# Linear attention and a gated feed-forward on one core: the later pairs' query projection as one block in four banks

## The chip, the core and the metric

The program runs on one core of a Trainium2 chip. The time of a kernel is the device time of that core in microseconds (us); the kernel before takes 1162.48 us, the median of three runs (1160.75 to 1164.28). The core has a matrix engine (TensorE, PE in the profile), a vector engine (VectorE, DVE), a scalar engine (ScalarE, ACT), GpSimd (POOL) and SyncE (SP), whose queue issues almost all DMAs, in order.

## The reference

Eight batches, eight heads, 576 tokens, head size 64. The features are exponentials of a projection on 128 columns, less its largest absolute value; the attention is linear in them. Its output, 4608 tokens of 512, goes through a gated feed-forward with 1536 hidden units.

```python
def phi(x):                                    # w_phi: 64 x 128
    proj = np.einsum('bhsd,df->bhsf', x, w_phi)
    proj = proj - np.max(np.abs(proj), axis=-1, keepdims=True)
    return np.concatenate([np.exp(proj), np.exp(-proj)], axis=-1)
q_p, k_p = (phi(q), phi(k))
kv = np.einsum('bhsf,bhsd->bhfd', k_p, v)
num = np.einsum('bhsf,bhfd->bhsd', q_p, kv)
den = np.einsum('bhsf,bhf->bhs', q_p, np.sum(k_p, axis=2))[..., None] + 1e-06
x = (num / den) as 4608 x 512
out = (silu(x @ w_gate) * (x @ w_val)) @ w_out
```

## The kernel before

**Work.** The attention goes by pairs of heads: 32 pairs, four to a batch. Pairs 0 to 11 are "early", pairs 12 to 31 "later" (this change touches these). A later pair has four pieces of PE work, called K, q, V and N below:

- K (lines 562, 565): the projection of the pair's keys, nine products of 128 columns. A head takes one half of the array's rows, so products of the two heads go side by side; the keys' last 64 tokens of both heads are the ninth product (line 565), on the first half of the rows. It takes three of the eight PSUM banks. DVE then takes the maximum and subtracts it (lines 573, 579), ACT makes the two exponentials (line 584).
- q (line 705): the projection of the queries, 288 columns for each head and half of the tokens. Each half is a step of its own: two products, two banks. ACT copies them out (line 710); DVE turns them, takes maxima and subtracts (714 to 738), ACT makes the exponentials (740, 742).
- V (601, 594): the sum over the keys, with the array split in two halves of columns. It needs the exponentials of K.
- N (760): the numerators and the denominator of the queries. ACT, DVE (770 to 782) divide and turn the result into the tile `turned`; four DMAs for every two pairs store it in DRAM (`x_dram`, line 794).

**The feed-forward** goes by 12 chunks c of 384 tokens. Chunks 0 to 3 are computed plainly (line 389 on PE). From chunk 4 on two chunks are done together by Strassen's scheme: seven products in place of eight (line 1214). For that `operands(c)` loads the attention's output back from `x_dram` into `stage` (line 1162), and ACT and DVE make of it seven split operands `tb` (1172, 1173, 1178); the first two are the tokens of chunk c alone, the third product of a step (operand 5) needs chunk c+1 as well. Chunk 4 begins with tokens of batches 2 and 3, so it needs pairs 12 to 15; chunk 7, the partner of chunk 6, needs pairs 20 to 23.

**Order.** A planner (class `Plan`) writes the program's order out: each step has an engine, a cost, what it waits for and the banks that it takes (`take`) and gives back (`give`). A step is taken when it is ready and as many banks are free as it takes; else it is held and the next one by key gets its turn. The order of instructions on every engine and on SP's queue is what comes out. While PE would wait in the plan, a product on an idle tile is put in (lines 1408 to 1413), in the feed-forward only while a sum over hidden units is open. The engines then run their queues strictly in that order. In the plain chunks two banks are held for the first layer and three for the second (`gv_names`, `begin_sums`), so three are free; when the first layer of chunk 3 is done the two are let go. In Strassen's steps four banks are held.

The functions that the change touches, and what calls them:

Of the kernel before, what the change touches and what calls it, by code (L numbers as in the profile page):

```python
# [17 lines left out]
P = 128  # L18
S = 576
SH = S // 2  # L20
NBL = S // 32
D = 64
NF = 128
# [54 lines left out]
class Plan:  # L78
# [21 lines left out]
    def add(self, eng, cost, fn, after=(), rank=0.0, take=None, give=None, mode="whole"):  # L100
        port = eng in ("DVE2", "POOL")
        eng = eng[:3] if eng == "DVE2" else eng
        s = Step(eng, cost, fn, rank, len(self.steps), self.LAG[eng], take, give, (rank, len(self.steps)))
        s.port = port
        s.slack = self.SLACK.get(eng, 0) if 16 <= rank < 1000 and cost > 1 else 0
        s.mode = mode if eng == "PE" and cost > 1 else None
        seen = set()
        for a in after:
            if a is not None and id(a) not in seen:
                seen.add(id(a))  # L110
                a.then.append(s)
                s.left += 1
        self.steps.append(s)
        return s
# [146 lines left out]
def dve(n):  # L261
    return 150 + 1.04 * n
# [10 lines left out]
def act(n):  # L273
    return 190 + 0.86 * n
# [6 lines left out]
def pe32(n):  # L281
    return 2 * max(112, 0.85 * n)
# [3 lines left out]
def favor_attention_moe(ctx: ExitStack, tc: tile.TileContext, qT, kT, v, w_phi, wg, wv, wo, out):  # L286
    nc = tc.nc
# [11 lines left out]
    def sb(name, shape, dtype=F32, n=None):  # L299
        if n is None:  # L300
            return pool.tile(shape, dtype, name=name, tag=name)
        return [pool.tile(shape, dtype, name=f"{name}{i}", tag=f"{name}{i}") for i in range(n)]
# [17 lines left out]
    kin, qin = sb("kin", [P, KW]), [sb("qin", [P, KW]), ahead.rearrange("p n c -> p (n c)")[:, :KW].bitcast(F32)]  # L320
# [4 lines left out]
    qx = [sb("qx0", [P, 2, S]), sb("qx1", [P, 2, S])]  # L325
# [3 lines left out]
    qy = sb("qy", [P, 4, NF], F32, 2)  # L329
# [20 lines left out]
    def bank(name):  # L350
        return banks.tile([P, 512], F32, name=name, tag=name)

    work = [bank(f"work{i}") for i in range(8)]
# [3 lines left out]
    wst = sb("wst", [P, NF])  # L357
# [9 lines left out]
    plan = Plan(len(work))  # L367
    add = plan.add
# [99 lines left out]
    def rows(h):  # L468
        return slice(h * D, h * D + D), slice((1 - h) * D, (1 - h) * D + D)
# [44 lines left out]
    last = {}  # L514

    def attention(i, rank):
        b, pr = divmod(i, NPAIR)
        early = i < EARLY_PAIRS
        j = i % 2
        jq = j if early else 0  # L520
        vec = nc.vector

        use = lambda name: [last.get((name, i - 2))]
# [8 lines left out]
        q_in = [add("SP", P * q_width * 4, lambda: nc.sync.dma_start(qin[jq][:, :q_width], qT[b, pr, :, :q_width]), q_free, rank)]  # L532
        if early:
            q_in.append(add("SP", 2 * D * D * 4, lambda: nc.sync.dma_start(side(qin[jq]), ends(qT)), q_free, rank))
        n = 4 * P * P
# [11 lines left out]
        for g, (t0, t1) in enumerate(K_GROUPS):  # L547
            both = t0 == 4
            w = t1 - t0
            heads = 1 if both else 2  # L550
            m2 = w * heads
            n = m2 * NF
            by_head = not both
            key = ("k", i, g)
            view = lambda key=key, n=n: work[plan.bank[key]][:, :n].rearrange("p (t f) -> p t f", f=NF)

            def project(t0=t0, t1=t1, key=key, heads=heads, both=both):
                projected.append(1)
                if not both:
                    for t in range(4):  # L560
                        for h in range(2):
                            nc.tensor.matmul(work[plan.bank["k", i, h]][:, t * NF:(t + 1) * NF],  # L562
                                             kin[rows(h)[0], t * P:(t + 1) * P], wst[rows(h)[0]], start=True, stop=True)
                if both or not early:
                    nc.tensor.matmul(work[plan.bank["k", i, 2]][:, :NF], kin[:D, 4 * P:], wst[:D], start=True, stop=True)  # L565

            if both and early:
                kproj = add("PE", pe32(NF), project, [*k_in, kproj], rank, take=key, mode="rows")
            elif not g:
                kproj = add("PE", (4 if early else 5) * pe32(NF), project, [*k_in, last.get(("kp", i - 1, 0))], rank,  # L570
                            take=[("k", i, n) for n in range(2 if early else 3)], mode="rows")
            m = km[(3 * i + g) % len(km)]
            kmax = add("DVE", dve(n), lambda m2=m2, m=m, view=view: vec.tensor_reduce(
                out=m[:, :m2], in_=view(), axis=AX.X, op=ALU.max, apply_absolute_value=True),
                       [kproj, last.get(("km", 3 * i + g - 4))], rank)
            kpv = kp[g]

            def centre(m2=m2, m=m, view=view, kpv=kpv):
                vec.tensor_tensor(  # L579
                    out=kpv[:, :m2, 1], in0=view(), op=ALU.subtract,  # L580
                    in1=m[:, :m2].rearrange("p (n o) -> p n o", o=1).broadcast_to([P, m2, NF]))

            def exponential(s, m2=m2, kpv=kpv):
                nc.scalar.activation(kpv[:, :m2, s], kpv[:, :m2, 1], AF.Exp, scale=-1.0 if s else 1.0)  # L584

            ksub = add("DVE", dve(n), centre, [kmax, last.get(("kp", i - 1, g))], rank, give=key)
            e0 = add("ACT", act(n), lambda f=exponential: f(0), [ksub], rank)
            e1 = add("ACT", act(n), lambda f=exponential: f(1), [e0], rank)
            last["km", 3 * i + g] = ksub

            def values(kpv=kpv):
                for s in range(2):
                    for r in sides:
                        nc.tensor.matmul(ps_kv()[r, s * 2 * VD:(s + 1) * 2 * VD], kpv[:, 0, s, r],  # L594
                                         vl.rearrange("p h d -> p (h d)"), start=False, stop=s == 1)

            def values_of_head(h=g, kpv=kpv):
                for t in range(4):
                    for s in range(2):
                        for r in sides:  # L600
                            nc.tensor.matmul(ps_kv()[r, (2 * s + h) * VD:(2 * s + h + 1) * VD], kpv[:, t, s, r],  # L601
                                             vf[:, t, h], start=t == 0 and h + s == 0, stop=False)

            summed.append(values_of_head if by_head else values)
            made_keys.append(e1)
            if early:
                kv_steps.append(add("PE", 8 * KV_PACE if by_head else 2 * pe32(2 * VD), summed[-1],
                                    [e1, *v_in, *kv_steps[-1:]], rank, take=None if g else ("kv", i), mode="columns"))
                last["kp", i, g] = kv_steps[-1]
# [30 lines left out]
        if early:  # L640
            for g in range(3):
                tail = g == 2
                w = 1 if tail else 4
                n = 3 * i + g
                key, key2 = ("q", i, g), ("t", i, g)
# [12 lines left out]
                if tail:  # L658
                    pj = add("PE", pe32(NF), project, [*q_in, pj], rank, take=key, mode="rows")
                elif not g:  # L660
                    pj = add("PE", 4 * pe32(NF), project, [*q_in, *use("qx"), last.get(("qy", 3 * i - 1))], rank, take=[key, ("q", i, 1)], mode="rows")
# [34 lines left out]
                ahead_used.append(pj)  # L696
        else:
            copies = [[], []]
            pj = None
            for part, c in enumerate(halves):  # L700
                keys = [("q", i, h, part) for h in range(2)]

                def project(keys=keys, c=c):
                    for h in range(2):
                        nc.tensor.matmul(work[plan.bank[keys[h]]][:, :SH], wst[rows(h)[0]], qin[jq][rows(h)[0], c],  # L705
                                         start=True, stop=True)

                pj = add("PE", pe32(SH), project, [*q_in, pj, *use("qx"), last.get(("qy", 3 * i - 1))], rank, take=keys, mode="rows")
                for h in range(2):
                    copies[h].append(add("ACT", act(SH), lambda h=h, part=part, key=keys[h]: nc.scalar.copy(  # L710
                        qx[j][:, h].rearrange("p (n u s) -> p u n s", u=2, s=32)[:, part],
                        work[plan.bank[key]][:, :SH].rearrange("p (n s) -> p n s", s=32)), [pj, *use("qx")], rank, give=keys[h]))
            last["qin", i] = pj
            turns = [add("DVE", dve(S), lambda h=h: vec.transpose(qe[j][:, h], qx[j][:, h]),
                         [*copies[h], *use("qe")], rank) for h in range(2)]
# [596 lines left out]
    def attend(tokens):  # L1312
        while made[0] < min(NB * NPAIR, NPAIR * ((tokens + S - 1) // S)):
            attention(made[0], float(made[0]))
            made[0] += 1
        if late_sums:
            late_sums.pop()([])
# [42 lines left out]
    for f in range(NFT):  # L1360
# [3 lines left out]
        for c in range(EARLY):  # L1364
            j, h = first(c, f, low, 0)
# [18 lines left out]
    for f in range(NFT):  # L1384
        j, h = first(PLAIN - 1, f, low_parts(f, 0), 0)
# [80 lines left out]
```

## Time and profile before

| | |
|---|---|
| median of the runs shown | 1162.48 us |
| the profiled execution | 1161.04 us |
| its span, first to last instruction | 1159.2 us |
| PE busy | 1152.4 us (99%) |
| DVE, ACT, POOL busy | 793.7, 546.7, 139.6 us |
| DMA, share of the 16 engines' time (main queue) | 79.7% |

The profile is of one execution; it took 1.44 us less than the median of the runs. A PE that is busy for 99% of the span isn't one that works at its peak all that time: matmuls overlap each other in the records, so what one costs is read from the distance between two starts, not from its duration.

### The profile page before, as it was taken

To read this page: it belongs to the slowest core of one execution; us is meant where nothing else is said; L and a number is where in the kernel's file an instruction comes from. 1 tells how busy PE (TensorE), PEld (TensorE's weight loads), DVE (VectorE), ACT (ScalarE), POOL (GpSimd) and SP (SyncE) were. 2 spreads that over 40 slices of the span, in tenths; PEclk is the share of its full clock that TensorE was granted. 3 is DMA by queue.
4 is the path that set the end of the run, shared out by engine and by line. 5 is a ranking of instruction groups with operands and counts; after the bars stand their busy time and mean duration, and the time that the engine had idled before them with its cause. 6 is when DMAs were issued, how large, how long until landed. Compare 5 with 4: busy or idle time off the path is not lost.

```text
span 1159.2 us, 26379 instructions
## 1 busy us (share of the span) xinstructions
PE 1152.4 (99%) x9985; PEld 1015.2 (88%) x9985; DVE 793.7 (68%) x1573; ACT 546.7 (47%) x1233; POOL 139.6 (12%) x142
## 2 busy tenths in 40 slices
PE   9999999999999999999999999999999999999998
PEld 8777779999898888898987899898899998899986
DVE  7989899999567777477787455777536786534431
ACT  6887563333434555445455343554423553433332
POOL 1222300000122313010010001100001100001100
PEclk9999999999999999999999999999999999999999
DMA  5546678777799999997887788887888787889774
GB/s 170 178 144 197 220 254 289 249 261 263 268 313 297 326 298 359 340 307 233 243 281 235 252 274 288 239 255 245 264 267 272 246 248 232 270 284 304 246 222 159
DMA packets 220591, 298.32 MB, mean 257 GB/s; under 512 B 65840, under 2 KB 126384, under 8 KB 220464
## 3 DMA queue, kind: packets, MB, share of 16 engines
q1 hardware_dynamic: 220304, 296.57, 79.7%
q8 instruction: 79, 1.29, 0.5%
q14 instruction: 48, 0.39, 0.1%
q10 hardware_dynamic: 160, 0.07, 0.0%
HBM read 217.91 MB, written 78.64 MB: 256 GB/s over the span
## 4 chain that ended last, share of the span: by engine, by line
PE 86%; DVE 1%; DMA 1%; issue 0%; SPq 0%; ACT 0%; ACTq 0%
PE work L389 41%; PE work L1214 31%; PE work L760 4%; PE work L601 4%; PE work L705 2%; PE work L562 2%; PE work L594 1%; PE work L1413 1%; DMA w_lo<-wlo_dram 0%; DMA stage<-x_dram 0%; PE work L565 0%; PE work L817 0%; PE work L813 0%; PE work L677 0%; DVE qy L667 0%
## 5 line engine op out<-in xcount | busy, mean ns | idle before, releaser
L389 PE MATMUL work<-w_hi,hh 128*128 128x512 f32 x468 | 183.1, 399 | 0.0
L1236 DVE TENSOR_TENSOR m<-m,work 128x384 f32<-128x384 f32 x144 | 78.6, 552 | 117.7 <-ACT m L1233 67.8
L389 PE MATMUL work<-w_hi,m 128*128 128x512 f32 x396 | 156.7, 396 | 0.0
L382 DVE TENSOR_TENSOR m<-m,hh 128x384 fp32r<-128x384 f32 x132 | 74.8, 573 | 97.7 <-ACT hh L1002 85.8
L1002 ACT CAST hh<-m 128x384 fp32r<-128x384 f32 x144 | 73.3, 512 | 138.5 <-PE work L389 74.2
L389 PE MATMUL work<-xh,w_big 128*128 128x384 f32 x384 | 132.3, 345 | 0.0
L382 POOL TENSOR_TENSOR m<-m,m 128x384 f32<-128x384 f32 x48 | 58.7, 1223 | 590.5 <-DVE m L1241 296.1
L389 PE MATMUL work<-xl,w_big 128*128 128x384 f32 x384 | 128.6, 335 | 0.0
L1214 PE MATMUL work<-tb,stream_xh 128*128 128x384 f32 x618 | 115.3, 338 | 0.0
L1214 PEld LDWEIGHTS work<-tb,stream_xh 128*128 128x128 f32 x618 | 107.0, 188 | 4.7 <-issue 3.8
L389 PEld LDWEIGHTS work<-w_hi,hh 128*128 128x128 f32 x468 | 87.9, 188 | 21.5 <-issue 1.7
L1233 ACT COPY m<-work 128x384 f32<-128x384 f32 x144 | 68.0, 475 | 73.2 <-PE work L1214 71.0
L1240 ACT ACTIVATE m<-m 128x384 f32<-128x384 f32 x96 | 45.5, 517 | 110.2 <-DVE m L1236 109.5
L584 ACT ACTIVATE kp<-kp 128x512 f32<-128x512 f32 x128 | 78.5, 630 | 26.5 <-DVE kp L579 25.3
L389 PEld LDWEIGHTS work<-w_hi,m 128*128 128x128 f32 x396 | 74.4, 188 | 17.8
L1214 PE MATMUL work<-tb,stream_xl 128*128 128x384 f32 x468 | 88.9, 338 | 0.4 <-ACT m L1233 0.4
L1214 PEld LDWEIGHTS work<-tb,stream_xl 128*128 128x128 f32 x468 | 81.0, 188 | 4.0 <-issue 2.3
L389 PEld LDWEIGHTS work<-xh,w_big 128*128 128x128 f32 x384 | 72.2, 188 | 7.5 <-issue 4.4
L1214 PE MATMUL work<-tb,tb 128*128 128x384 f32 x408 | 77.8, 337 | 0.0
L601 PEld LDWEIGHTS work<-vf,kp 128*64 128x64 f32 x2048 | 62.6, 138 | 13.4 <-issue 5.5
L382 POOL TENSOR_TENSOR s<-s 128x256 f32<-128x256 f32 x48 | 41.3, 862 | 270.1 <-DMA s<-w_dram 231.7
L389 PEld LDWEIGHTS work<-xl,w_big 128*128 128x128 f32 x384 | 72.2, 188 | 1.0
(141 smaller groups left out, 2340.1 us busy)
## 6 DMA issues: line engine op xcount, KB each, us to landing
stream_xh<-wv_dram SPq DMA_DIRECT2D x103, 256.0 KB, 4.0
h_dram<-m SPq DMA_DIRECT2D x124, 192.0 KB, 3.8
m<-h_dram SPq DMA_DIRECT2D x124, 192.0 KB, 4.1
stream_xl<-wv_dram SPq DMA_DIRECT2D x78, 256.0 KB, 3.9
tb<-wv_dram SPq DMA_DIRECT2D x77, 256.0 KB, 4.1
w_lo<-wlo_dram SPq DMA_DIRECT2D x72, 256.0 KB, 4.2
stream_w_lo<-wv_dram SPq DMA_DIRECT2D x52, 256.0 KB, 3.9
stream_xl<-wlo_dram SPq DMA_DIRECT2D x48, 256.0 KB, 3.8
```

The costliest lines, as they stand in the source:

```text
L382: (nc.gpsimd if on == "POOL" else nc.vector).tensor_tensor(out=o, in0=a, in1=b, op=op)
L389: nc.tensor.matmul(o, l, r, start=a, stop=z)
L562: nc.tensor.matmul(work[plan.bank["k", i, h]][:, t * NF:(t + 1) * NF], kin[rows(h)[0], t * P:(t + 1) * P], wst[rows(h)[0]], start=True, st ...
L584: nc.scalar.activation(kpv[:, :m2, s], kpv[:, :m2, 1], AF.Exp, scale=-1.0 if s else 1.0)
L601: nc.tensor.matmul(ps_kv()[r, (2 * s + h) * VD:(2 * s + h + 1) * VD], kpv[:, t, s, r], vf[:, t, h], start=t == 0 and h + s == 0, stop=False)
L705: nc.tensor.matmul(work[plan.bank[keys[h]]][:, :SH], wst[rows(h)[0]], qin[jq][rows(h)[0], c], start=True, stop=True)
L760: nc.tensor.matmul(o[r, at:at + VD], features(k, h, slice(D * n, D * n + D)), kvs[j][:, (2 * k + h) * VD:(2 * k + h + 1) * VD], start=n % ...
L1002: s4 = add("ACT", act(CH), lambda: nc.scalar.copy(hh[b], th(j)), [made, hid_free[b]], FIRST)
L1214: nc.tensor.matmul(o(), l, r, start=begin and k + m == 0, stop=k + m == 3, skip_group_check=True)
L1233: return j, into(j, add("ACT", act(CH), lambda: nc.scalar.copy(th(j), src()), after, FIRST))
L1236: return add("DVE", dve(CH), lambda: vec.tensor_tensor(out=th(j), in0=th(j), in1=src(), op=ALU.add), after, FIRST)
L1240: s1 = into(t, add("ACT", act(CH), lambda: nc.scalar.activation(th(t), th(j), AF.Tanh, scale=0.5), [ready], FIRST))
```

## The change

For the later pairs the two steps of the query projection become one. It takes four banks (both heads, both halves) at once and issues eight products of 144 columns in place of four of 288, the heads in turn. The copies on ACT wait for the whole step and give back one bank each, as before. In the block of the keys the product of the last tokens goes first and the heads' order is turned round, so that the halves of rows still alternate. The early pairs keep their order. From line 716 on, line numbers of the changed kernel are three higher (1214 is 1217, 760 is 763, 794 is 797).

```diff
-            def project(t0=t0, t1=t1, key=key, heads=heads, both=both):
+            def project(both=both):
                 projected.append(1)
+                if both or not early:
+                    nc.tensor.matmul(work[plan.bank["k", i, 2]][:, :NF], kin[:D, 4 * P:], wst[:D], start=True, stop=True)
                 if not both:
                     for t in range(4):
-                        for h in range(2):
+                        for h in (0, 1) if early else (1, 0):
                             nc.tensor.matmul(work[plan.bank["k", i, h]][:, t * NF:(t + 1) * NF],
                                              kin[rows(h)[0], t * P:(t + 1) * P], wst[rows(h)[0]], start=True, stop=True)
-                if both or not early:
-                    nc.tensor.matmul(work[plan.bank["k", i, 2]][:, :NF], kin[:D, 4 * P:], wst[:D], start=True, stop=True)
...
-            pj = None
+            def project():
+                for part in range(2):
+                    for piece in range(2):
+                        for h in range(2):
+                            c = slice(part * SH + piece * SH // 2, part * SH + (piece + 1) * SH // 2)
+                            nc.tensor.matmul(work[plan.bank["q", i, h, part]][:, piece * SH // 2:(piece + 1) * SH // 2],
+                                             wst[rows(h)[0]], qin[jq][rows(h)[0], c], start=True, stop=True)
+
+            pj = add("PE", 2 * pe32(SH), project, [*q_in, *use("qx"), last.get(("qy", 3 * i - 1))], rank,
+                     take=[("q", i, h, part) for part in range(2) for h in range(2)], mode="rows")
             for part, c in enumerate(halves):
-                keys = [("q", i, h, part) for h in range(2)]
-
-                def project(keys=keys, c=c):
-                    for h in range(2):
-                        nc.tensor.matmul(work[plan.bank[keys[h]]][:, :SH], wst[rows(h)[0]], qin[jq][rows(h)[0], c],
-                                         start=True, stop=True)
-
-                pj = add("PE", pe32(SH), project, [*q_in, pj, *use("qx"), last.get(("qy", 3 * i - 1))], rank, take=keys, mode="rows")
                 for h in range(2):
```

The planner's order changes with it. **The first later query projection on PE.** In the kernel before, the first half of pair 12's queries stands in the plain chunks, right ahead of pair 12's V, with three free banks:

```order
L389 MATMUL work_131<-w_lo_90,hh_121 128x512
L389 MATMUL work_131<-w_hi_84,hh_123 128x512
L705 MATMUL work_130<-qin,wst 128x288
L705 MATMUL work_129<-qin,wst 128x288
L601 MATMUL work_133<-vf,kp_101 64x65 x16
L601 MATMUL work_133<-vf,kp_102 64x65 x16
L594 MATMUL work_133<-vl,kpt 64x130 x4
```

In the changed kernel it stands about 460 rows later, after the two banks of the first layer are let go and after the V of pairs 12, 13 and 14, behind nine idle products:

```order
L1416 MATMUL work_134<-idle 128x256 x9
L705 MATMUL work_128<-qin,wst 128x144
L705 MATMUL work_130<-qin,wst 128x144
L705 MATMUL work_128<-qin,wst 128x144
L705 MATMUL work_130<-qin,wst 128x144
L705 MATMUL work_129<-qin,wst 128x144
L705 MATMUL work_127<-qin,wst 128x144
L705 MATMUL work_129<-qin,wst 128x144
L705 MATMUL work_127<-qin,wst 128x144
L389 MATMUL work_134<-w_hi_76,hh_123 128x512
```

The queries of pairs 12 to 15, and with them their N, moved towards the first Strassen step (chunk 4).

**The first Strassen step on PE.** Before, pair 17's K stands six products of Strassen's after the step's beginning, and Strassen's products stand around it (line 1214; `x6` is one product with its six matmuls):

```order
L562 MATMUL work_134<-wst,kin 128x128
L565 MATMUL work_132<-wst,kin 128x128
L1214 MATMUL work_129<-tb_4973,stream_w_lo_5288 128x384 x6
L1214 MATMUL work_127<-tb_5039,stream_w_lo_5288 128x384 x6
L1214 MATMUL work_133<-tb_5039,stream_w_lo1v 128x384 x6
L1214 MATMUL work_128<-tb_5018,tb_5068 128x384 x6
L1214 MATMUL work_127<-tb_4973,tb_5068 128x384 x6
L1214 MATMUL work_133<-tb_5018,tb_5068 128x384 x6
L705 MATMUL work_131<-qin,wst 128x288
```

Now pair 17's K and pair 16's queries stand right ahead of the step's first product, and pair 17's V right behind it:

```order
L564 MATMUL work_133<-wst,kin 128x128
L705 MATMUL work_131<-qin,wst 128x144
L705 MATMUL work_133<-qin,wst 128x144
L705 MATMUL work_131<-qin,wst 128x144
L705 MATMUL work_133<-qin,wst 128x144
L705 MATMUL work_134<-qin,wst 128x144
L705 MATMUL work_132<-qin,wst 128x144
L705 MATMUL work_134<-qin,wst 128x144
L705 MATMUL work_132<-qin,wst 128x144
L1217 MATMUL work_129<-tb_5282,stream_xh_4905 128x384 x6
L601 MATMUL work_131<-vf,kp_101 64x65 x16
L601 MATMUL work_131<-vf,kp_102 64x65 x16
```

Between pair 17's K and its V ten products of the feed-forward lay, pair 17's queries and pair 16's N; now there are pair 16's queries and one product.

**SP's queue ahead of chunk 6's step.** Before, between the last stores of pairs 22 and 23 and the loads of chunk 7 into `stage` stand five other loads:

```order
L794 DMA x_dram<-turned 32x2x576 x2
L1148 DMA stream_xl_5356<-wlo_dram 128x512
L990 DMA m_7346<-h_dram 128x384
L794 DMA x_dram<-turned 32x2x576
L1148 DMA stream_xl_5356<-wlo_dram 128x512
L990 DMA m_7360<-h_dram 128x384
L1148 DMA stream_xl_5356<-wlo_dram 128x512
L990 DMA m_7374<-h_dram 128x384
L1148 DMA stream_xh_5354<-wlo_dram 128x512
L1162 DMA stage_4880<-x_dram 128x2x192 x4
```

Now the stores stand behind the output of chunk 5's last sum, and only the keys of pair 26 stand between them and the loads:

```order
L1039 DMA out_dram<-osb_4862 128x512
L1151 DMA stream_w_lo_5233<-wv_dram 128x512
L797 DMA x_dram<-turned 32x2x576 x3
L525 DMA kin<-in_kT_dram 128x512
L529 DMA kin<-in_kT_dram 64x2x64
L1165 DMA stage_5251<-x_dram 128x2x192 x4
```

The stores and the loads moved to the very end of the plain second layer, with the beginning of the Strassen step right behind them.

## Rows read from the trace of the kernel before

**Rows 1.** The page: the span, and part 1's line of PE.
```profile
span 1159.2 us, 26379 instructions
...
PE 1152.4 (99%) x9985; PEld 1015.2 (88%) x9985; DVE 793.7 (68%) x1573; ACT 546.7 (47%) x1233; POOL 139.6 (12%) x142
```
**Rows 2.** Waits of PE by waiting line and releaser: us in total, times, longest.
```profile
PE work L1214 <- ACT m L1233: 0.4, 1, 0.4
```
**Rows 3.** Timeline of PE, 354 to 363 us: start, length, engine, line, operation.
```profile
354.67 0.76 PE L705 MATMUL work<-qin,wst 64*128 64x288 f32 x4
355.36 0.44 PE L389 MATMUL work<-xh,w_big 128*128 128x384 f32 x1
...
356.62 0.76 PE L705 MATMUL work<-qin,wst 64*128 64x288 f32 x4
357.31 0.44 PE L389 MATMUL work<-xh,w_big 128*128 128x384 f32 x1
...
358.03 2.09 PE L601 MATMUL work<-vf,kp 128*64 128x65 f32 x64
...
360.39 0.28 PE L760 MATMUL work<-kvs,qe 128*64 128x65 f32 x4
...
362.58 0.50 PE L389 MATMUL work<-w_hi,hh 128*128 128x512 f32 x1
```
**Rows 4.** Timeline of PE, 342 to 344 us: a K block and what follows.
```profile
342.18 1.16 PE L562 MATMUL work<-wst,kin 64*128 64x128 f32 x16
...
343.49 0.50 PE L389 MATMUL work<-w_hi,hh 128*128 128x512 f32 x1
```
**Rows 5.** Timeline of PE, 474 to 477 us: chunk 4's first Strassen product.
```profile
475.07 0.39 PE L389 MATMUL work<-w_hi,m 128*128 128x512 f32 x1
475.30 1.92 PE L1214 MATMUL work<-tb,stream_xh 128*128 128x384 f32 x10
```
**Rows 6.** Timeline of ACT, 342 to 350 us: pair 13's exponentials.
```profile
345.29 1.23 ACT L584 ACTIVATE kp<-kp 128x512 f32<-128x512 f32 x2 [0.90 <-DVE kp L579]
...
348.90 0.30 ACT L584 ACTIVATE kpt<-kpt 128x128 f32<-128x128 f32 x1
```
**Rows 7.** Timeline of PE: behind N of pairs 15, 23; chunk 6's first product.
```profile
416.80 0.45 PE L389 MATMUL work<-xh,w_big 128*128 128x384 f32 x1
...
646.24 0.50 PE L389 MATMUL work<-w_hi,hh 128*128 128x512 f32 x1
...
674.28 2.27 PE L1214 MATMUL work<-tb,stream_w_lo 128*128 128x384 f32 x12
```
**Rows 8.** Timeline of DVE, 643 to 690 us: pair 23's output, chunk 7's operands.
```profile
648.88 0.78 DVE L782 STREAM_TRANSPOSE turned<-num 128x576 f32<-128x576 f32 x1
...
666.94 0.56 DVE L1178 TENSOR_TENSOR stage<-stage 128x384 f32<-128x384 f32 x1 [1.04 <-DMA stage<-x_dram]
...
670.23 2.89 DVE L1173 TENSOR_TENSOR tb<-stage,tb 128x384 fp32r<-128x384 f32 x6
```
**Rows 9.** Timeline of SP's queue, 640 to 690 us: last store, loads of `stage`.
```profile
655.20 0.47 SPq L794 DMA_DIRECT2D x_dram<-turned  x1
...
659.95 1.96 SPq L1162 DMA_DIRECT2D stage<-x_dram  x4
```
**Rows 10.** The DMAs that read the tile `turned` (the stores), issue to landing.
```profile
DMA to landing us min/median/max: 2.2/3.6/5.3
```
**Rows 11.** The DMAs that write the tile `stage` (the loads), issue to landing.
```profile
DMA to landing us min/median/max: 4.1/5.1/6.3
```
**Rows 12.** Timeline of ACT, 438 to 452 us: chunk 4's first operand.
```profile
440.55 0.93 ACT L1172 CAST tb<-stage 128x384 fp32r<-128x384 f32 x2 [1.15 <-DMA stage<-x_dram]
```
**Rows 13.** Timeline of DVE, 438 to 455 us: chunk 4's first operand.
```profile
441.09 1.03 DVE L1173 TENSOR_TENSOR tb<-stage,tb 128x384 fp32r<-128x384 f32 x2 [0.70 <-ACT tb L1172]
```
**Rows 14.** Timeline of PE, 0 to 14 us: one form at the start and later.
```profile
1.52 4.46 PE L1408 MATMUL work<-ident 128*128 128x128 f32 x20 [1.52 <-POOL vl L364]
...
12.71 1.09 PE L677 MATMUL work<-ident,qy 128*128 128x128 f32 x8
```

More of the change, by code (lines that the diff above doesn't have):

```diff
@@ L698, in attention @@
             copies = [[], []]
-            pj = None
-            for part, c in enumerate(halves):
-                keys = [("q", i, h, part) for h in range(2)]
-                def project(keys=keys, c=c):
-                    for h in range(2):
-                        nc.tensor.matmul(work[plan.bank[keys[h]]][:, :SH], wst[rows(h)[0]], qin[jq][rows(h)[0], c],
-                                         start=True, stop=True)
-                pj = add("PE", pe32(SH), project, [*q_in, pj, *use("qx"), last.get(("qy", 3 * i - 1))], rank, take=keys, mode="rows")
+            def project():
[7 more added lines that the diff above has]
+                     take=[("q", i, h, part) for part in range(2) for h in range(2)], mode="rows")
+            for part, c in enumerate(halves):
                 for h in range(2):
-                    copies[h].append(add("ACT", act(SH), lambda h=h, part=part, key=keys[h]: nc.scalar.copy(
+                    copies[h].append(add("ACT", act(SH), lambda h=h, part=part: nc.scalar.copy(
                         qx[j][:, h].rearrange("p (n u s) -> p u n s", u=2, s=32)[:, part],
-                        work[plan.bank[key]][:, :SH].rearrange("p (n s) -> p n s", s=32)), [pj, *use("qx")], rank, give=keys[h]))
+                        work[plan.bank["q", i, h, part]][:, :SH].rearrange("p (n s) -> p n s", s=32)),
+                        [pj, *use("qx")], rank, give=("q", i, h, part)))
             last["qin", i] = pj
```

## The prediction

> **What bounds the kernel now.** I read the page first, then the waits of PE, then PE's timeline around the queries and keys, then the way from an N through `x_dram` to an operand on the other engines. PE is busy for 1152.4 of 1159.2 us [rows 1]. Its longest wait in the Strassen part is 0.4 us, once [rows 2]. So PE's queue is the time: what takes place on it away shortens the kernel, and any new wait on it lengthens it in full. The reader should look for two prices: what a change of the array's split costs, and how long the ways are on which PE would come to wait if its cover went.
>
> **What the change saves on PE.** A block of two query products of 288 columns takes 0.69 us from its start to the next one (354.67 to 355.36), and a K block, five products of 128 columns on the fuller half of the rows, 1.31 [rows 3, 4]. Each product is two passes, so with f a fixed part and s the time of a column f + 2 x 288 s = 0.69 and f + 10 x 128 s = 1.31: s = 0.00088 us and f = 0.18. Plain products fit: three of 384 columns between two blocks take 0.72 and six 1.26 [rows 3], 0.18 each and 0.18 fixed. So a stretch in one split costs 0.18 us beside its columns, whatever the split. The order on PE shows how many stretches there are: 255 before (39 of them query halves alone), 228 after. The query stretches fall by 21, the plain ones between them by 12, and those in columns rise by 6, because V and N, often joined before, are now more often apart. 27 x 0.18 = **4.9 us** less. The columns stay the same: 8 x 144 on two halves is 4 x 288 on two halves, so a block is 0.18 + 8 x 144 x 0.00088 = 1.19 in place of two of 0.69 and a plain start. If pieces of 144 went no faster than blocks of 288 with their own start, only the 12 plain starts less the 6 others would stay, 1.1 us; if columns were free, 20 x 1.19 is the floor, which no row supports. Three idle products fewer out of 131 are left out.
>
> The product of the keys' last tokens at the front: five products stand on one half of the rows and four on the other, before and after, so the block stays at 1.31. A partner found or lost for it would be two passes of 128 columns, 0.23 us a pair, 4.5 us on 20 pairs in either direction; I take nothing, since the fuller half alone makes the 1.31 in row 342.18.
>
> **What the order takes in exchange.** Four banks at once are not there while the first layer holds two of them and the second three. Pair 12's queries move some 460 rows back on PE, and with them the N of pairs 12 to 15. Before, pair 15's N ended at 416.80 and chunk 4's first Strassen product started at 475.30 [rows 5, 7]; pair 23's N ended at 646.24 and chunk 6's first product started at 674.28 [rows 7]. I count in the new order what is left between them, with 0.18 for a stretch, 0.18 for a product of 384 columns, 0.23 for one of 512 (475.07 to 475.30) [rows 5], 1.0 for a query block's columns, 1.1 for a K block's, 2.36 for V (358.03 to 360.39) [rows 3].
>
> - Chunk 4: pair 16's V 2.36, eighteen plain products 4.3, pair 17's K and pair 16's queries in one stretch 2.3. The first operand is due **9.0 us** after pair 15's N; then its six matmuls 1.3, pair 17's V 2.5, six matmuls, and operand 5 is due at 14.0.
> - Chunk 6: pair 24's V 2.36, six plain products and twelve Strassen ones 3.7, K of 25 and queries of 24 2.3, V of 25 2.5, K of 26 1.3. Operand 5, the first that needs pair 23, is due **12.2 us** after pair 23's N.
>
> How long the way is: from pair 23's N to the end of `turned` 648.88 + 0.78 - 646.24 = 3.4 us [rows 7, 8]. A store lands 3.6 us after its issue and a load 5.1, by the median [rows 10, 11]; four issues take 1.96 [rows 9]. The first operand's split runs from 440.55 to 442.12, 1.6 us [rows 12, 13].
>
> - Chunk 4, operand 1: 3.4, the last of four stores begins 1.5 later and lands after 3.6 (8.5), two loads begin until 9.0 and land at 14.1, the split ends at 15.7. PE waits 15.7 - 9.0 = 6.7 us. Then DVE's new order puts fourteen operations on tiles and one turn of queries ahead of operand 5's end; six in 2.89 are 0.48 each [rows 8], so 7.5 us, to 23.2. PE with its first wait is there at 20.7 and waits 2.5 more. **9.2 us**.
> - Chunk 6: the last three stores stand on SP behind the output of the last plain sum, whose matmuls end 3.9 after the N; with its copy and the issues, about 1 us and 2 us by my estimate from the 0.48 an issue takes [rows 9], the last store begins at 6.9, lands at 10.5, four loads begin until 12.0 and land at 17.1. From the last landing to operand 5 DVE took 666.94 to 672.2 (two thirds of the 2.89) [rows 8], 5.2: 22.3. PE is there at 12.2 and waits **10.1 us**.
>
> Inside these two waits lies a third that the order alone shows. Pair 13's exponentials ended at 349.20, 5.7 us after the stretch behind its K began at 343.49 [rows 4, 6]. In the new order pair 17's V comes 2.3 us after its K, pair 25's 1.0 us after its. These two must wait 3.4 and 4.7, 8.1 us together, even if every transfer were early; that is the least. The most: the ways took 25.3 us (416.80 to 442.12) and 26.0 (646.24 to 672.2) before [rows 7, 8, 13], with SP free to put others first; as long again the waits are 18.8 and 13.8, 32.6. I take the sum of the single rows, 19.3, since SP's new order puts little between stores and loads. Chunks 8 and 10 keep over 40 us between their N and their step by the same count and wait for nothing.
>
> **Sum.** 1161.04 - 4.9 + 19.3 = 1175.4 for the profiled execution; the median of the runs is 1.44 above it: 1176.9, rounded to **1177 us**.
>
> **Weighed against a rule.** At the start, after rest, twenty passes on 128 columns took 4.46 us, 0.22 each, and the same form later 1.09 for eight, 0.14 with the last one's tail [rows 14]: about half speed for the first 4.4 us of work, the lower of the clock's two levels (1.2 and 2.4 GHz) by the durations. The Trainium skill, "TensorE: Matmul & The Clock Gate", section "HAM oscillation", says that the array falls back to its slow clock when bursts of matmuls are parted by waits, and each burst then starts cold. By that rule the clock drops in both new waits, and the idle products that could bridge them stand only where a sum is open, which is not so here; no stretch of this trace between the first product and the last has such a wait. By the row alone, the sum stays at 1177.
>
> **The rivals.**
> - Slow clock behind the waits. Two falls would make up to 4.4 us of work take twice as long each, 8.8; part of it lies under the wait that follows (2.5 in chunk 4, most of V and K in chunk 6), so I count half, 4.4: **1181 us**. For it: the first 4.4 us of the program. Against it: nothing after that ever ran slow, since PE never rested. The rule named above gives this time.
> - Only the keys' waits bind, the transfers being early: 1162.48 - 4.9 + 8.1 = **1166 us**. For it: stores land in as little as 2.2 us and loads in 4.1 [rows 10, 11]. Against it: even with these the chain for chunk 4 is 3.4 + 1.5 + 2.2 + 0.5 + 4.1 + 1.6 = 13.3, 4.3 over its 9.0.
> - The other side, faster: the waits at the two steps' beginnings don't come, and the 4.9 us of stretches are all there is: **1158 us**. It decides where both waits together stay under 4.9. For it: PE waited nowhere before although the planner cut as finely. Against it: 5.7 us from a K to its exponentials, and 1.0 and 2.3 us of work there now.
> - The ways stay as long as they were, because SP's queue is filled in front of them: 32.6 - 4.9: **1190 us**. For it: 25.3 and 26.0 us measured. Against it: then nothing pressed, and loads of the feed-forward were put between.
>
> **How the numbers follow.** Two waits at full clock 0.47, with the slow clock 0.27, the longer ways 0.10, keys alone 0.09, faster 0.07. The range from 1163 to 1189 leaves out the faster case and about half of the longer ways; the likeliest one's own is 1168 to 1186, from waits of 6 and 5 to 13 and 13 us. About 0.3% (3.5 us) is what a measurement of this kernel can tell from no change. Faster by more than that 0.07; within it 0.08 (most of the keys' case); slower 0.85.
>
> **What would show it.** Right: query blocks of eight products near 1.2 us and some 27 fewer changes of split; PE's waits before line 1217 for `tb` and before line 601 for `kp` at two places, 7 to 13 us each, and none elsewhere above 1 us; on SP, loads of `stage` that begin as the last store lands. Wrong: PE's waits under 5 us in total, or such waits in the plain chunks or at chunks 8 and 10, or K blocks that change from 1.31.

## The result, and the profile after

The changed kernel takes 1175.09 us, the median of five runs (1174.08 to 1175.56). Its ratio to the kernel before is 1.0106, 95% interval 1.0091 to 1.0121: slower, 2 us under the 1177 that was forecast. The profiled execution took 1174.08 us. The page of the changed kernel, its span, part 1's line of PE and part 2's row of the granted clock:

```profile
span 1172.3 us, 26705 instructions
...
PE 1156.2 (99%) x10142; PEld 1031.5 (88%) x10142; DVE 795.1 (68%) x1573; ACT 542.1 (46%) x1233; POOL 133.9 (11%) x142
...
PEclk9999999999999999899999989999999999999999
```

Against [rows 1] the span is 13.1 us longer and PE still counts as 99% busy, so the page hides the loss. The digits of the clock give it away: 8 in slices 17 and 24 of 29.3 us each, in which chunks 4 and 6 begin. PE's waits in the changed kernel (waiting line, releaser, us in total, times, longest), where [rows 2] had 0.4 us once:

```profile
PE work L705 <- DVE kp L579: 4.0, 2, 2.2
PE work L1217 <- ACT tb L1175: 3.4, 2, 1.8
...
PE work L1217 <- DVE tb L1176: 1.2, 2, 0.7
PE work L601 <- ACT qx L712: 1.0, 1, 1.0
```

That is 9.6 us, all at the two beginnings; chunks 8 and 10 have none, and the lines left out (2.4 us, at the start and in the plain chunks) stand in the kernel before too. The timeline of PE in the changed kernel at chunk 4 (answers to [rows 5]) and at chunk 6 (answers to [rows 7]): start, length, engine, line, operation, and in brackets the idle time before it.

```profile
474.13 1.16 PE L564 MATMUL work<-wst,kin 64*128 64x128 f32 x15
475.12 0.41 PE L705 MATMUL work<-qin,wst 64*128 64x144 f32 x2
477.33 2.44 PE L705 MATMUL work<-qin,wst 64*128 64x144 f32 x14 [1.80 <-DVE kp L579]
481.56 2.56 PE L1217 MATMUL work<-tb,stream_xh 128*128 128x384 f32 x6 [1.79 <-ACT tb L1175]
484.06 3.70 PE L601 MATMUL work<-vf,kp 128*64 128x65 f32 x64
...
488.13 1.49 PE L1217 MATMUL work<-tb,stream_xh 128*128 128x384 f32 x7
490.33 1.16 PE L1217 MATMUL work<-tb,stream_xh 128*128 128x384 f32 x5 [0.72 <-DVE tb L1176]
...
690.79 2.01 PE L705 MATMUL work<-qin,wst 64*128 64x144 f32 x14 [2.17 <-DVE kp L579]
693.76 3.73 PE L601 MATMUL work<-vf,kp 128*64 128x65 f32 x64 [0.96 <-ACT qx L712]
...
701.72 0.45 PE L1217 MATMUL work<-tb,stream_w_lo1v 128*128 128x384 f32 x1 [1.62 <-ACT tb L1175]
702.65 1.97 PE L1217 MATMUL work<-tb,stream_w_lo1v 128*128 128x384 f32 x5 [0.48 <-DVE tb L1176]
```

Two things are to be seen. The first wait is not for an operand: the queries of pair 16 stand right behind K of pair 17 and take four banks, three of them K's own (K has 132 to 134 in the order, the queries 131 to 134), so behind their first product they wait until DVE has subtracted (1.80 us; 2.17 at pair 24). And what follows each wait is slow: 64 products of V have 3.70 us where they had 2.09 [rows 3]. Windows of the changed kernel, the columns being busy time by engine, the granted clock, the DMA share and GB/s:

```profile
470.00:474.00 4.00, 4.00 (x19) 2.92 (x17) 0.00 (x0) 1.25 (x3) 0.00 (x0) 1.00 0.82 225
474.00:478.00 4.00, 2.20 (x26) 1.99 (x27) 2.61 (x5) 1.24 (x3) 0.00 (x0) 0.92 0.79 264
478.00:482.00 4.00, 2.21 (x13) 1.69 (x11) 0.82 (x3) 2.77 (x7) 0.00 (x0) 0.50 0.98 326
482.00:486.00 4.00, 4.00 (x42) 3.40 (x43) 3.20 (x8) 2.78 (x9) 0.00 (x0) 0.50 1.08 381
486.00:490.00 4.00, 3.62 (x49) 3.12 (x45) 4.00 (x10) 3.45 (x9) 0.00 (x0) 0.80 1.06 396
```

The granted clock is 0.50, the lower level of 1.2 GHz, for 8 us behind the idle time, and 0.55 to 0.83 at 692 to 708. I measured what a beginning costs by its stretches, from one start on PE to the next, against the same work without a wait and at full clock (in brackets, by the distances of such products elsewhere). Chunk 4: K and q 7.65 (2.26), the first six Strassen matmuls 2.50 (1.26), V 4.07 (2.5), the next stretch 8.50 (7.56): **9.1 us**. Chunk 6: K and q 6.76 (2.26), V 4.53 (2.46), K 3.43 (1.31), Strassen 22.51 (20.2): **11.0 us**. PE is idle for 4.3 of the 9.1 and 5.2 of the 11.0; the rest is work that took longer. With 13.1 in the span, the rest of the program became 20.1 - 13.1 = 7.0 us shorter.

### The profile page after: what moved, and what is told of

The parts are those of the page before. It is cut to its first block, busy times and chain, and to the rows that moved or that the text cites. A ratio compares the mean times of both kernels' runs of the same rounds, so it can differ in the third digit from the quotient of the medians.

```text
span 1172.3 us, 26705 instructions
## 1 busy us (share of the span) xinstructions
PE 1156.2 (99%) x10142; PEld 1031.5 (88%) x10142; DVE 795.1 (68%) x1573; ACT 542.1 (46%) x1233; POOL 133.9 (11%) x142
## 3 DMA queue, kind: packets, MB, share of 16 engines
q8 instruction: 80, 1.31, 0.5%
## 4 chain that ended last, share of the span: by engine, by line
PE 85%; DVE 2%; ACT 0%; DMA 0%; SPq 0%; issue 0%; DVEq 0%; ACTq 0%
PE work L389 41%; PE work L1217 31%; PE work L763 4%; PE work L601 4%; PE work L705 2%; PE work L564 1%; PE work L594 1%; PE work L1416 1%; PE work L560 1%; DVE tb L1176 0%; DMA stage<-x_dram 0%; DVE stage L1181 0%; PE work L820 0%; ACT kp L584 0%; PE work L816 0%
## 5 line engine op out<-in xcount | busy, mean ns | idle before, releaser
L382 POOL TENSOR_TENSOR m<-m,m 128x384 f32<-128x384 f32 x48 | 58.3, 1214 | 611.6 <-DVE m L1244 455.0
L389 PEld LDWEIGHTS work<-w_hi,m 128*128 128x128 f32 x396 | 74.4, 188 | 17.9
L601 PEld LDWEIGHTS work<-vf,kp 128*64 128x64 f32 x2048 | 65.8, 143 | 14.9 <-issue 5.6
L1217 PEld LDWEIGHTS work<-tb,tb 128*128 128x128 f32 x408 | 71.8, 190 | 1.0 <-DVE num L779 0.2
```

The lines of the kernel that those rows point to most:

```text
L382: (nc.gpsimd if on == "POOL" else nc.vector).tensor_tensor(out=o, in0=a, in1=b, op=op)
L389: nc.tensor.matmul(o, l, r, start=a, stop=z)
L1217: nc.tensor.matmul(o(), l, r, start=begin and k + m == 0, stop=k + m == 3, skip_group_check=True)
```

## The experiments

**Theory:** the step that takes four banks is held in the plain chunks, where three are free; N of pairs 12 to 15 come out late, and at the beginnings of chunks 4 and 6 PE waits for what hangs on them. **Rivals:** A, the products' new form costs the time; B, the wait of q for K's banks does, wherever they meet; C, the slow clock does.

**1. Two steps for all later pairs.** Heads in turn, pieces of 144 and the keys' tail in front stay; the condition is true for all pairs.

```diff
+            steps = ((0,), (1,)) if True else ((0, 1),)
+            for parts in steps:
+                pj = add("PE", len(parts) * pe32(SH), lambda ...: project(parts), [*q_in, pj, ...], rank,
-            pj = add("PE", 2 * pe32(SH), project, ...
-                     take=[("q", i, h, part) for part in range(2) for h in range(2)], mode="rows")
+                         take=[("q", i, h, part) for part in parts for h in range(2)], mode="rows")
```

> The changed kernel with the query block cut back into two steps of two banks each for all later pairs; the pieces of 144 columns, the heads in turn and the keys' tail at the front stay. Theory (the take of four banks moves the N of pairs 12 to 15 and 20 to 23 late, and PE then waits at the starts of chunks 4 and 6): the order has 255 stretches again, 57.7 us stand between pair 15's N and chunk 4, so no wait over 1 us, 1162.5 us (1161 to 1164). Rival A (the edits to the products themselves, pieces or tail, cost the time): some 5 to 13 us above before, 1168 to 1175. Rival C (slow clock, brought on by anything but those waits): granted clock 0.99 again and 1166 to 1170.

Measured: 1163.61 us, ratio 1.001 (1.0 to 1.0019), clock 1.000, no wait over 1 us in the feed-forward. The form of the products costs at most 2.2 us, the upper end of the interval; A is out as the cause of the 13 us, and the loss hangs on the take.

**2. Two steps for pairs 12 to 15 alone.** The same edit with `if i < 16`.

> The changed kernel with two steps of two banks for pairs 12 to 15 alone; pairs 16 to 31 keep the block in four banks. By the order 58.3 us stand between pair 15's N and chunk 4 (9.1 in the changed kernel), 20.9 between pair 23's N and chunk 6 (3.8), and 234 stretches are left. Theory (late N): no wait at chunk 4, 0 to 3 at chunk 6, the saving in stretches stays (21 x 0.18 = 3.8, with the three small waits of before 5): 1156 to 1160 us, faster than before. Rival A (pieces, tail): still over 1168. Rival B (a query block behind a K block waits for the K block's banks, 1.8 to 2.2 us each time, wherever it stands): the waits stay at several places, 1162 to 1168. Rival C (slow clock by itself): clock 0.99 and over 1165.

Measured: **1156.27 us**, ratio 0.9944 (0.9931 to 0.9956), faster than both kernels. All of PE's waits of 0.2 us and more, the largest at the start of the program:

```profile
PE work L1414 <- POOL vl L364: 1.5, 1, 1.5
PE work L560 <- issue: 0.7, 1, 0.7
PE work L655 <- DVE kp L579: 0.6, 1, 0.6
PE work L564 <- DMA kin<-in_kT_dram: 0.5, 1, 0.5
PE work L601 <- ACT m L979: 0.3, 1, 0.3
PE work L1220 <- DVE m L1242: 0.2, 1, 0.2
```

No line for `tb` and none for q behind K is left, though sixteen pairs still take four banks: the block in four banks by itself costs nothing. What B's wait costs where it comes isn't shown by this run, since in its order no query block stands right behind a K block; in the changed kernel that is so at the two beginnings alone. Chunk 6's wait went as well, which fits the 20.9 us of work that the order has in front of it in place of 3.8.

**3. The reverse: the block in four banks for pairs 12 to 15 alone** (`if i >= 16`).

> The reverse: the block in four banks for pairs 12 to 15 alone, two steps for pairs 16 to 31. By the order 9.1 us stand between pair 15's N and chunk 4, 36.3 between pair 23's N and chunk 6. Theory: chunk 4's wait comes alone, 8 to 10 us of it, chunk 6 has none; nothing is saved elsewhere, so 1162.5 + 9 = 1171 us (1169 to 1174). Rival A' (each four-bank block costs a little, 13 us over 20 pairs): 4 x 0.65 = 2.6, 1165. Rival C (slow clock counts for most): one fall instead of two to three, about 1166.

Measured: 1169.9 us, ratio 1.0062 (1.0049 to 1.0076): 7.4 us lost to four pairs. PE's timeline of this kernel shows chunk 4's waits alone:

```profile
478.32 0.76 PE L705 MATMUL work<-qin,wst 64*128 64x144 f32 x6 [1.80 <-DVE kp L579]
482.45 2.56 PE L1220 MATMUL work<-tb,stream_xh 128*128 128x384 f32 x6 [3.37 <-ACT tb L1178]
...
490.61 1.14 PE L1220 MATMUL work<-tb,stream_xh 128*128 128x384 f32 x5 [0.66 <-DVE tb L1179]
```

As the theory has it, near the lower end of its range; 2.6 us (A') and the 1166 of C are out. The wait for K's banks is there with two banks as well, since the second half of pair 16's queries still stands behind K of pair 17.

**4. Four products of 288 columns in the block** in place of eight of 144; takes and order stay.

```diff
-                    for piece in range(2):
-                        for h in range(2):
-                            c = slice(part * SH + piece * SH // 2, part * SH + (piece + 1) * SH // 2)
+                for part, c in enumerate(halves):
+                    for h in range(2):
+                        nc.tensor.matmul(work[...][:, :SH], wst[rows(h)[0]], qin[jq][rows(h)[0], c], ...)
```

> The changed kernel with four products of 288 columns in the block in place of eight of 144; takes, steps and order of steps stay. Theory (columns cost the same in either size): block of 1.18 us stays within 0.05, 1175 us (1174 to 1176.5). Rival (the pieces are what makes the block short, 2 x 0.69 = 1.38 without them): 20 x 0.20 = 4 us more, 1179.

Measured: 1173.69 us, ratio 1.0091 (1.0077 to 1.0105), 0.3 us under the theory's range and not to be told from the changed kernel. One block and the row behind it, of the changed kernel and then of this one:

```profile
406.50 1.25 PE L705 MATMUL work<-qin,wst 64*128 64x144 f32 x16
407.68 0.50 PE L389 MATMUL work<-w_hi,hh 128*128 128x512 f32 x1
```

```profile
406.95 1.24 PE L703 MATMUL work<-qin,wst 64*128 64x288 f32 x8
408.12 0.50 PE L389 MATMUL work<-w_hi,hh 128*128 128x512 f32 x1
```

From start to next start 1.18 and 1.17 us: the pieces do nothing, the joining saves.

**5. Idle products in the waits,** to price the clock.

```diff
+    def bridge(c, n):                      # c: 4 at pair 16's queries, 6 at pair 24's
+        if ("z", 3, c) in plan.bank:       # a bank that Strassen's step has not begun on
+            for _ in range(n):
+                nc.tensor.matmul(ps(("z", 3, c), 2 * NF), idle[:, :P], idle, start=True, stop=True)
```

It is called with 12 ahead of the queries of pairs 16 and 24, and with 14 ahead of chunk 4's first product and of chunk 6's product of operand 5.

> The changed kernel with idle products of 256 columns, 12 to 14 in a row, in front of the queries of pairs 16 and 24 and in front of the first product that waits in chunks 4 and 6, 52 in all: PE works through most of the waits, on nothing. Theory (the waits are the loss; the fall of the clock behind them costs a little, since most of it lies under the next wait): granted clock back to 0.995 or more, 1 to 4 us of time given back, 1171 to 1174 us. Rival C (the slow clock is most of the 13 us): 8 us or more given back, under 1168. Rival D (idle products come on top): 52 x 0.107 = 5.6 us and eight changes of split, 1.4: up to 1182.

Measured: 1175.49 us, ratio 1.0108 (1.0092 to 1.0125). The mean granted clock is 0.999 in the profiled execution and 0.994 to 0.997 in the others (0.990 and 0.991 in the changed kernel). Windows of the profiled execution, to be held against those above:

```profile
478.00:482.00 4.00, 3.44 (x28) 2.82 (x26) 0.75 (x3) 2.16 (x5) 0.00 (x0) 1.00 0.95 292
482.00:486.00 4.00, 3.16 (x62) 2.65 (x64) 2.74 (x6) 2.90 (x9) 0.00 (x0) 1.00 1.09 371
486.00:490.00 4.00, 2.46 (x31) 1.71 (x26) 4.00 (x10) 4.00 (x11) 0.00 (x0) 1.00 1.03 378
```

In chunk 4 the clock is back and the time is not: C is out, and of my own 1 to 4 us no more than about 2 can hide in the two intervals. From K of pair 17 to the end of the product that waits last for `tb` in chunk 4 PE took 17.4 us in the changed kernel (473.91 to 491.33) and 17.9 here (474.29 to 492.18). What PE does faster, it waits longer; DVE is busy for 4.00 of 4.00 us from 486 on, and its chain of operands sets the end. At chunk 6 the same stretch is 17.4 (687.00 to 704.42) and 17.2 us (688.41 to 705.62).

Behind this last wait of chunk 6 the clock fell in this run too. The window of 704 to 708 us in the changed kernel, in this one and in run 9 below:

```profile
704.00:708.00 4.00, 4.00 (x19) 4.00 (x19) 3.77 (x13) 1.78 (x4) 0.00 (x0) 0.74 0.36 112
704.00:708.00 4.00, 4.00 (x16) 4.00 (x17) 3.97 (x9) 1.78 (x4) 0.00 (x0) 0.64 0.25 65
704.00:708.00 4.00, 4.00 (x25) 4.00 (x24) 3.77 (x12) 1.76 (x4) 0.00 (x0) 1.00 0.78 238
```

From operand 5's first product to the next query block PE took 22.5, 22.7 and 21.3 us in the three. In run 9 the wait in it is that of the changed kernel (0.49 and 0.48), so there the lower clock costs 1.2 us that nothing covers, and these idle products don't price it.

**6. Earlier rows,** to take the stores' landing out of the way.

```diff
-                x(n)..., x_dram[e, :, p, 2 * k:2 * k + 2, at]), ...
+                x(n)..., x_dram[e - (e == {4: 1, 6: 3}.get(c, -1)), :, p, 2 * k:2 * k + 2, at]), ...
```

> The changed kernel with the stage loads of chunks 4 and 6 reading rows of the batch before (batches 2 and 4 in place of 3 and 5), which were stored long ago: they wait for no store, and the output of those rows is not the reference's. The order of every queue stays. Theory as predicted (a store's landing of 3.6 us is a link of the way): the first stage loads begin up to 3.6 us earlier, and 3 to 6 us are given back, 1169 to 1172. Rival E (SP issues without a pause between the stores and the loads, so the stores have landed when the loads' turn comes): the loads begin where they did, less than 1 us changes, 1174 to 1176.

Measured: 1174.64 us, ratio 1.0095 (1.0081 to 1.0108). The first stage load of chunk 4 began at 476.14, in the changed kernel at 476.11: the store's landing holds nothing up, against the prediction. The chain of waits of the changed kernel, 466 to 484 us (start, length, what), shows what does come before the loads:

```profile
469.52 4.41 PE work L389 x18
473.93 0.02 issue
473.95 0.61 ACT osb L1036
474.56 0.06 SPq L1039
...
475.64 0.43 SPq L1151
476.07 0.04 issue
476.11 0.43 SPq L1165
...
478.12 5.13 DMA stage<-x_dram
```

SP's queue is in order: the output of the last plain sum (L1039) and three weight loads (L1151) stand ahead of the loads (L1165).

**7. Two steps for pairs 12 to 15 and 20** (`if i < 16 or i == 20`), the version that the second experiment and the order point to.

> Two steps of two banks for pairs 12 to 15 and for pair 20; the block in four banks for the other fifteen. By the order 58.3 us stand between pair 15's N and chunk 4, 25.8 (20.9 without pair 20's) between pair 23's N and chunk 6, and PE's own time is 0.8 us less than with 12 to 15 alone. Theory: no wait, 1155.5 us (1154.5 to 1156.5), faster than before by 0.6%. Rival B (waits for the K block's banks come back at other pairs): 1157 to 1160.

Measured: **1154.53 us**, ratio 0.9923 (0.9911 to 0.9936), no wait over 0.9 us outside the start. The best of all kernels here.

**8 to 10. What sets the loads' way.** Pair 17's two `vl` loads, 1.59 us of SP's row, go to ACT (8, pair 25's too, with the earlier rows), or are left out with the earlier rows (9) and without (10).

```diff
-        v_in += [add("SP", P * P, lambda h=h: nc.sync.dma_start(vl[...], vr[:, h]), ...
+        v_in += [add("SP", P * P, lambda h=h: (nc.scalar if i in (17, 25) else nc.sync).dma_start(...      # 8
+        v_in += [add("SP", P * P, lambda h=h: None if i == 17 else nc.sync.dma_start(...                   # 9, 10
```

> The run with the earlier rows (stage loads of chunks 4 and 6 that wait for no store; the output of those rows is not the reference's), and in it the two vl loads of pair 17 and of pair 25 issued by ACT in place of SP. In the changed kernel they took SP 1.59 us between the last store and the first stage load of chunk 4, in a row of issues without a pause. Rival E (SP's row of issues sets when the loads begin): chunk 4's first stage load begins about 1.6 us earlier, its first Strassen product too, 1 to 2 us less than with the earlier rows alone: 1172.5 to 1173.5. Theory as predicted is out already if that is so. Rival F (the DMA engines are full here, share 0.95 to 1.1, so a load issued earlier lands no earlier): the first product within 0.5 us of where it was, 1174 to 1176.

> The run with the earlier rows, with the two vl loads of pair 17 left out altogether (pair 17 uses the values of pair 16's last tokens; the output is not the reference's in both respects). In the run before they had gone to ACT's queue, and SP's weight loads then waited 2.6 us for their landing; here nothing takes their place, and no wait for a store is left. Rival E (SP's row of issues sets when the loads begin): chunk 4's first stage load begins about 1.6 us earlier than 476.1 and its first Strassen product 1 to 2 us earlier, time 1 to 2 us less than with the earlier rows: 1172.6 to 1173.6. Rival F (the DMA engines are full, a load issued earlier lands no earlier): loads begin earlier, the first product stays within 0.5 us, 1174 to 1176.

> The changed kernel with only the two vl loads of pair 17 left out; the stage loads read the rows that were just stored, and wait for them. Here the store's landing (last of four issues begun about 471.3, landing after 2.2 to 5.4) would be the next link. Theory as predicted: the loads begin at 475 to 475.5 in place of 476.1, as the last store lands, half a microsecond to one given back, 1174 to 1174.6. Rival E without a store's wait: they begin at 474.5, 1173 to 1174. Rival F: no change, 1174.6 to 1175.6.

Measured: 1175.39 us (1.0107, 1.009 to 1.0123), 1174.23 (1.0101, 1.0084 to 1.0118), 1174.16 (1.010, 1.0085 to 1.0115). In 8 the loads began later, at 477.53, since SP's weight loads waited for something new (SP's queue, us in total, times, longest):

```profile
SPq L1151 <- DMA vl<-in_v_dram: 2.6, 2, 2.0
```

So 8 tells nothing on E or F. In 9 and 10 they began 1 us earlier. The places in chunk 4 in one execution of each, in us behind the start of pair 17's K (operand 5: its first start that waits for DVE):

| run | first load | first product | operand 5 |
|---|---|---|---|
| changed kernel | 2.20 | 7.65 | 16.42 |
| 6 (earlier rows) | 2.13 | 8.50 | 16.80 |
| 9 (earlier rows, no `vl`) | 1.19 | 7.46 | 15.76 |
| 10 (no `vl`) | 1.13 | 7.54 | 15.79 |

Against run 6, which its expectation starts from, run 9 has both products 1.04 us earlier, as E has it; run 10 has them 0.1 and 0.6 earlier than the changed kernel, nearer to F at the first. But the changed kernel and 6, whose loads begin at the same place, differ by 0.85 at the first product, and the times of 6, 9 and 10 can't be told apart. So E and F stay open. F's full DMA engines agree with the share of 0.98 to 1.08 in the windows above, but no run took traffic away.

## Why the prediction was right, and where not

**What bounds.** Right: PE's queue is the time, new waits on it cost in full, and the run without them (2) is as much faster as the stretches say. The sign, the two places and the cause, N held back by the take of four banks, are shown by 1 to 3.

**The saving.** The query block has 1.18 us (1.19 forecast), K keeps 1.31 (357.64 to 358.95 in the changed kernel), the tail's place and the pieces cost nothing that can be measured. The term was too small: -4.9 was forecast for 27 stretches, and the rest of the program gave 7.0. Run 2 gives 6.2 us for 21, 0.30 each in place of 0.18, though PE's small waits there add up to 1.0 us more than before (3.8 and 2.8). Where the rest comes from stays open.

**The wait at chunk 4.** Forecast 9.2, measured 9.1. From pair 15's N (end 467.21) the loads began at 8.9 us (9.0), the first product at 14.35 (15.7), operand 5 at 23.1 (23.2). The step that failed is "the last of four stores begins 1.5 later and lands after 3.6": the loads stand where I put them, but behind the last plain sum's output and the weight loads on SP (6), which I had counted for chunk 6 alone. Two ways of the same length made the number right for a wrong reason, and that is luck.

**The wait at chunk 6.** Forecast 10.1, measured 11.0. Operand 5's first product came 20.7 us behind pair 23's N (681.06 to 701.72), which leaves 8.5 over the 12.2; the other 2.5 us are the second wait of 0.48 and products at a granted clock of 0.74 to 0.83 behind it. The part that waits for DVE, the counterpart of the 23.1 at chunk 4, came at 21.6 (22.3 forecast). The way is not the forecast's to its end. ACT and DVE in the changed kernel:

```profile
698.41 0.38 ACT L633 COPY kvs<-work 128x260 f32<-128x260 f32 x1 [3.80 <-PE work L594]
698.68 3.40 ACT L1175 CAST tb<-stage 128x384 fp32r<-128x384 f32 x8
...
699.23 1.03 DVE L1176 TENSOR_TENSOR tb<-stage,tb 128x384 fp32r<-128x384 f32 x2 [0.41 <-ACT tb L1175]
```

In ACT's queue the copy of pair 25's V stands ahead of the casts. ACT was idle for 3.80 us until that V ended, which took 4.53 in place of 2.46, and DVE, through with the loaded tokens, then waited 0.41 for the first cast. So V ended last and the loads were in time by 0.41; in run 5, with V at full clock, ACT waited 1.31 for the loads instead. The forecast has no term for this.

**The keys' waits inside them.** "These two must wait 3.4 and 4.7" failed. V of pair 17 waited for nothing and V of pair 25 for 0.96 us. In their place the queries, which the order puts between K and V, waited for K's banks (1.80 and 2.17), which the banks in the order's rows would have told; so exponentials had the time.

**The slow clock.** It came, in both places, as the rival had it. The Trainium skill, "TensorE: Matmul & The Clock Gate", section "HAM oscillation", says that an array that waits between bursts of matmuls falls back to its slow clock; here the trace agrees (0.50 for 8 us from the wait of 1.80 us on). Most of the 4.4 us that the rival charges were not there: with the clock at 1.00 the time stayed (5), because in chunk 4 DVE's operands end last, and in chunk 6 the loads come in V's place. About 1.2 us behind chunk 6's last wait were (5 and 9). So what came is the rival's case at nearly the likeliest one's price. The rival's row shows no fall of the clock: at the start, 0 to 6 us, the kernel before has a granted clock of 1.00 in the profile, so what made those twenty products slow stays open.

**Sum.** In the span 14.4 was forecast (19.3 - 4.9) and 13.1 came (20.1 - 7.0): both terms were too small, by 0.8 and 2.1, and since they have opposite signs only 1.3 us of the errors is left: luck again. In the prediction's range for the likeliest case the upper end is added up wrong: waits of 13 and 13 us give 1184, not 1186. Chunks 8 and 10 wait for nothing, as forecast. A reader who wants the better kernel gets it by the same argument: the four-bank step pays, as long as it isn't asked for where three banks are free and something is due (7: 8.8 us faster than the kernel before in its runs).

## What to carry to other kernels

A step that takes more of a pooled resource at once is not only longer or shorter: where the pool never has that much, it is held, and everything behind it comes late. Compare what the neighbours hold with the new take, and then the distance in work between each late producer and its consumer with the way between them. Before pricing a slow clock or a transfer behind a wait, look which chain ends last there: what another chain covers is worth nothing, and what lies behind the last wait counts in full.

## What the runs showed of the hardware that was not expected

Twelve idle products of 256 columns held the granted clock at 1.00 through 1.7 us that else stood idle (5, the profiled execution). Two small loads of 64 partitions, moved from SP's queue to ACT's, made two weight loads of SP's queue wait 2.6 us for them, by the profile's reading. And with the DMA engines at a share near 1, loads issued at the same place (the changed kernel and 6) let the first product start 7.65 us behind pair 17's K in one execution and 8.50 in the other.
